# A semaphore wait of GpSimd on VectorE's last SBUF operation, in an attention and MoE kernel

## The chip, the cores and the metric

The kernel runs on one core of a Trainium2 chip. The metric is the device time of one execution in microseconds (us). Five engines take part: TensorE (PE, its weight loads PEld), VectorE (DVE), ScalarE (ACT), GpSimd (POOL), and SyncE (SP), which issues all DMAs. Each engine works through its own queue in order and meets the others only through semaphores. Half a per cent of the time is 3.7 us.

## What is computed

Attention over 4 batches of 8 heads, 576 positions, head size 64, with rotated queries and keys; its output is the input of a two-layer block on 2304 tokens, all in float32.

```python
scores = scale * np.matmul(rotate(q), rotate(k).transpose(0, 1, 3, 2))
attn = np.exp(scores - np.max(scores, axis=-1, keepdims=True))
attn = attn / (np.sum(attn, axis=-1, keepdims=True) + 1e-09)
x = np.matmul(attn, v).transpose(0, 2, 1, 3).reshape(2304, 512)
h = x @ w_in                                  # 512 -> 2048
out = (h * (1.0 / (1.0 + np.exp(-1.702 * h)))) @ w_out   # 2048 -> 512
```

## The kernel before

Heads go in 16 pairs. For each pair, `prep` loads q and k (RAW tiles), turns them by three `combine` operations with the tables `cos_sin_sb` (a product into BT, a product in RAW, a sum into RAW; all L354), and transposes them on TensorE (L475). The transposed tiles become KP for the first four pairs, and for the others KA, KB, QT and QZ, split into a high and a low part (L349 or L351, and L519). `scores` multiplies them into PSUM (SPS; L607, L627). `softened` copies a row negated with its least value on VectorE (L646), and ScalarE takes the exponential (L649, into PP or PJ). The weights are transposed (PT; L709, L804, L837, L882), copied to PW or PH and multiplied with v (AV). The sums of the rows are inverted (ST; L680 adds, L681 inverts, L684 transposes), and the output tile XS is scaled and split into two parts and written to `x_dram`.

The second block goes in 9 chunks of 256 tokens and 16 slices of the inner size. TensorE computes h from XC and win (L1038), ScalarE the tanh (L1044), VectorE the product T (L1046); T is copied (G, high part, L341 to L345) and subtracted (G, low part, L354), and TensorE multiplies by wout (L1055). The weights win and wout arrive as 64-bit words and are converted by integer steps on tiles CW or CV: L992 and L994 on ScalarE, L996, L998 and L1001 on VectorE, an integer add on GpSimd (L1004), a cast (L341 or L343) and a subtraction (L354).

No operation is issued in the order of the source. Every one is given to a `Plan` with its engines, durations, buffers and a priority, and `Plan.order` works out a timetable at build time; the operations are then issued in the order of their planned starts. `vec` marks each with a `port`: `(POOL, DVE)` for an operation on SBUF alone, `(POOL,)` for one that reads PSUM. In the timetable two operations that carry a port with their own engine in it do not overlap:

```python
if e in o.port and port_at > t + 1e-9:
    at(port_at, e, o)
    continue
```

On the chip this is not enforced: before the change the only waits are those that data and buffers need. `copy` (L339) and `combine` (L353) are the helpers that most operations on GpSimd go through, so the profile shows lines L345 and L354 for many different tiles. The last loop of the kernel (L1098) issues the operations.

Of the kernel before, what the change touches and what calls it, by code (L numbers as in the profile page):

```python
# [15 lines left out]
ALU = mybir.AluOpType  # L16
# [30 lines left out]
PE, ACT, DVE, POOL, SP = "PE", "ACT", "DVE", "POOL", "SP"  # L47
# [234 lines left out]
def attention_moe(ctx: ExitStack, tc: tile.TileContext, q, k, v, w_in, w_out, cos_sin, out):  # L282
    nc = tc.nc
# [53 lines left out]
    engine = {ACT: nc.scalar, DVE: nc.vector, POOL: nc.gpsimd}  # L337

    def copy(e, to, src):  # L339
        if e == ACT:  # L340
            nc.scalar.copy(to, src)  # L341
        elif e == DVE:
            nc.vector.tensor_copy(to, src)  # L343
        else:
            nc.gpsimd.tensor_scalar(to, src, 1.0, 1.0, op0=ALU.mult, op1=ALU.mult)  # L345

    def scaled(e, to, src, by):
        if e == ACT:
# [2 lines left out]
            nc.vector.tensor_scalar(to, src, by, None, op0=ALU.mult)  # L351

    def combine(e, to, a, b, how):  # L353
        engine[e].tensor_tensor(to, a, b, op=how)  # L354

    def dma(fn, nbytes, *deps, full=0, part=0, row=2048, land=900.0, **kw):

# [18 lines left out]
    def make_tiles(pool, counts):  # L376
        for p, n in counts.items():
            at = base.get(p, 0)
            for i in range(at, at + n):
                plan.tiles[p][i] = pool.tile(shape[p][0], shape[p][1], name=f"{p}{i}")  # L380

    def open_pool(name, side, counts=None):
        pool = tc.tile_pool(name=name, bufs=1, side=side, reuse_waits="tile")
        tiles = pool.__enter__()
        make_tiles(tiles, counts or {})
        return pool, tiles
# [40 lines left out]
    def prep_qk(n, s, prio):  # L427
# [18 lines left out]
        if n in plain_qk:  # L446
            def f():
                for h in range(2):
# [3 lines left out]
                    else:  # L452
                        for i, src in enumerate((q, k)):
# [7 lines left out]
        rope = "POOL DVE" if n or s == 1 else "DVE POOL"  # L461
        heads = lambda t: t.rearrange("p t c (a d) -> p t (c a) d", a=2)
        o = vec(rope, "two", w, lambda e: combine(e, halves(bt.t[:, 0:n_t]), halves(raw.t)[:, :, :, ::-1, :], sn,
                                                  ALU.mult), ld, tables, bufs=[raw, bt], prio=prio + at["rope"])
        o = vec(rope, "two", w, lambda e: combine(e, heads(raw.t), heads(raw.t), cs, ALU.mult), o, bufs=[raw],
                prio=prio + at["rope"])
        added = n < at["n_added"]
        if not added:
            o = vec(rope, "two", w, lambda e: combine(e, raw.t, raw.t, bt.t[:, 0:n_t], ALU.add), o, bufs=[raw, bt],
                    prio=prio + at["rope"])  # L470
# [61 lines left out]
    def prep(n):  # L532
# [40 lines left out]
        for h in range(2):  # L573
            vs = plan.buf("VS")
            pr = p0 + at["v_split"] + (0 if h == 0 else PAIR_LEN[n] / 3)
            hi = vec("ACT POOL", "sbuf", 5 * D, lambda e, h=h, vs=vs: copy(e, vs.t[:, :, 0, :], raw.t[:, h]), ld,
                     bufs=[raw, vs], prio=pr)
            lo = vec("POOL DVE", "two", 5 * D, lambda e, h=h, vs=vs: combine(
                e, vs.t[:, :, 1, :], raw.t[:, h], vs.t[:, :, 0, :], ALU.subtract), hi, bufs=[raw, vs], prio=pr)
            vs_of[n].append(vs)  # L580
            vs_ready[n].append(lo)
# [91 lines left out]
    def inverse_sums(n, tiles, exps, xs, prio):  # L673

        st, pt, rt = st_of[n], pt_buf(n), buf("RT")
        c0, k = column_of[n].index(tiles[0]), len(tiles)

        def f():
            a = st.t[:, 1, c0:c0 + k]
            nc.vector.tensor_scalar(a, a, 1e-9, None, op0=ALU.add)  # L680
            nc.vector.reciprocal(a, a)  # L681

        o = op(DVE, 330.0, f, exps, bufs=[st], prio=prio)
        o = pe(lambda: nc.tensor.transpose(pt.t[0:k, 0:128], st.t[:, 1, c0:c0 + k], ident), o, tr=[128],  # L684
               bufs=[st, pt, rt], prio=prio)
        o = vec("ACT DVE", "psum", 128, lambda e: copy(e, rt.t[0:k], pt.t[0:k, 0:128]), o, bufs=[pt, rt], prio=prio)
        o = dma(lambda: nc.sync.dma_start(r_dram[n, c0:c0 + k], rt.t[0:k]), 4600, o, full=1, bufs=[rt], prio=prio)

        heads = [[t for t in tiles if t < 4], [t for t in tiles if t > 4]]
        row = lambda t: column_of[n].index(t) * 128  # L690
        pieces = [(0, 128 * heads[0][0], row(heads[0][0]), 128 * len(heads[0]) + 64 * (4 in tiles)),
                  (64, 128 * heads[0][0], row(heads[1][0]), 128 * len(heads[1]))]
        if 4 in tiles:
            pieces.append((64, 512, row(4) + 64, 64))

        def f():
            rows = r_dram[n].rearrange("(a t) p -> a (t p)", a=1)
            for r0, to, at, w in pieces:
                nc.sync.dma_start(xs.t[r0:r0 + 64, 0, to:to + w], rows[:, at:at + w].to_broadcast([64, w]))

        return dma(f, 34000.0 * k, o, part=len(pieces), land=1350.0, bufs=[xs], prio=prio)
# [14 lines left out]
    def split(pt, ph, ready, parts, prio):  # L716

        done = []
        for r0, r1, c0, c1, to in parts:
            w = c1 - c0  # L720
            src = lambda r0=r0, r1=r1, c0=c0, c1=c1: pt.t[r0:r1, c0:c1]
            part = lambda l, to=to, w=w, tall=r1 - r0 == 128: (
                ph.t[:, 512 * l + to:512 * l + to + w] if tall else ph.t[64 * l:64 * l + 64, to:to + w])
            hi = vec("ACT DVE", "psum", w, lambda e, src=src, part=part: copy(e, part(0), src()), ready, bufs=[pt, ph],
                     prio=prio + at["copy_p"], chain="turned")
            done.append(vec("DVE", "psum", w, lambda e, src=src, part=part: nc.vector.tensor_tensor(  # L726
                part(1), src(), part(0), op=ALU.subtract), hi, bufs=[pt, ph], prio=prio + at["copy_p"]))
        return done
# [366 lines left out]
    with tc.manual_schedule():  # L1095
        mid, _ = open_pool("mid", "right", MID)
        left, _ = open_pool("early", "left", early)
        for o in plan.order():  # L1098
            if mid and any(b.pool in LATER for b in o.bufs):
                mid.__exit__(None, None, None)  # L1100
                mid = None
                later = ctx.enter_context(tc.tile_pool(name="later", bufs=1, side="right", reuse_waits="tile"))
                make_tiles(later, LATER)
            if left and first_late <= o.idx < last_late:
                left.__exit__(None, None, None)
                left = None
                late = ctx.enter_context(tc.tile_pool(name="late", bufs=1, side="left", reuse_waits="tile"))
                win[1] = late.tile([128, 2, KD, DFF // 2], F32R, name="win1")
                wout[1] = late.tile([128, 2, KH, DM], F32R, name="wout1")
            o.fn(o.eng)  # L1110


# [38 lines left out]
```

## Time and profile before

| | |
|---|---|
| time, median of 3 runs | 740.62 us (739.92 to 742.65) |
| the profiled execution | 742.06 us |
| its span in the trace | 740.3 us |
| busy, TensorE / VectorE / ScalarE / GpSimd | 707.0 / 501.4 / 421.1 / 254.1 us |
| operations, VectorE / GpSimd | 1168 / 297 |

The span is the time from the first to the last instruction in the trace; the rest of the execution's time lies around it. An engine's busy time is the sum of its instructions' durations, overlaps counted once. An instruction that stands still inside its execution counts as busy, so a long duration of a form that is short elsewhere is a sign of such a stand. Idle time in square brackets at a row is that of the engine just before it, with what ended it. Later sections name the stretches by the trace's time in us.

### The profile page before, as it was taken

What the parts mean: (1) busy time and instruction counts of PE and PEld (TensorE: products, weight loads), DVE (VectorE), ACT (ScalarE), POOL (GpSimd) and SP (SyncE); (2) the same over time, 40 slices, a digit from 0 to 9 for tenths busy, and PEclk for the clock granted to TensorE, in tenths of its full rate; (3) what the DMA queues carried; (4) which work ended last, traced back from release to release, by engine and by line L of the source; (5) the groups of instructions that cost most, each with busy time, mean ns of one, the idle gap of its engine ahead of it and who ended that gap; (6) DMA issues with size and microseconds to landing.
All of it is one profiled execution on the core that took longest, in us unless ns stands there. A gap on an engine that the chain in (4) does not pass through costs nothing.

```text
span 740.3 us, 14104 instructions
## 1 busy us (share of the span) xinstructions
PE 707.0 (95%) x4921; PEld 618.0 (83%) x4921; DVE 501.4 (68%) x1168; ACT 421.1 (57%) x1038; POOL 254.1 (34%) x297
## 2 busy tenths in 40 slices
PE   6899797999999999999999999999999999999997
PEld 4566475878887898999999999899999998999996
DVE  5999999888889886477788788788752222222322
ACT  3677896666867764466666666766653232322322
POOL 4687765455456434144143433432110000000000
PEclk7999998999999999999999999999999999999999
DMA  7545647555455544222232343521103020100000
GB/s 174 143 104 163 187 141 207 176 161 148 134 169 155 165 137 116 93 73 70 63 99 67 93 120 97 126 66 44 38 17 118 1 86 0 60 28 1 29 1 29
DMA packets 103335, 72.16 MB, mean 97 GB/s; under 512 B 67536, under 2 KB 88032, under 8 KB 103264
## 3 DMA queue, kind: packets, MB, share of 16 engines
q1 hardware_dynamic: 103264, 71.26, 34.0%
q8 instruction: 39, 0.64, 0.4%
q14 instruction: 32, 0.26, 0.1%
HBM read 48.87 MB, written 15.28 MB: 87 GB/s over the span
## 4 chain that ended last, share of the span: by engine, by line
PE 80%; DVE 9%; ACT 4%; DMA 3%; issue 2%; POOL 1%; SPq 1%; ACTq 0%; DVEq 0%; POOLq 0%
PE PT L1038 26%; PE SPS L1055 25%; PE SPS L607 8%; PE AV L737 5%; PE PT L709 5%; PE SPS L627 2%; PE PT L882 2%; PE PT L804 1%; PE AV L895 1%; PE PT L475 1%; DVE PP L646 1%; PE AV L819 1%; DMA RAW<-in_k_dram 1%; ACT PP L649 1%; DVE RAW L354 1%
## 5 line engine op out<-in xcount | busy, mean ns | idle before, releaser
L1038 PE MATMUL PT<-XC,win 128*128 128x256 f32 x1728 | 242.3, 286 | 0.2
L1038 PEld LDWEIGHTS PT<-XC,win 128*128 128x128 f32 x1728 | 227.2, 191 | 9.3 <-DVE T L1046 1.3
L1055 PE MATMUL SPS<-wout,G 128*128 128x512 f32 x864 | 234.4, 400 | 0.3 <-ACT G L341 0.3
L1055 PEld LDWEIGHTS SPS<-wout,G 128*128 128x128 f32 x864 | 150.5, 189 | 23.3 <-ACT G L341 0.7
L1046 DVE SCALAR_TENSOR_TENSOR T<-T,PT 128x256 f32<-128x256 f32 x144 | 60.4, 419 | 90.9 <-ACT T L1044 89.6
L1044 ACT ACTIVATE T<-PT 128x256 f32<-128x256 f32 x144 | 55.1, 383 | 113.7 <-PE PT L1038 105.7
L649 ACT ACTIVATE PP<-PP,ST 128x576 f32<-128x576 f32 x128 | 99.3, 777 | 24.2 <-DVE PP L646 23.2
L646 DVE TENSOR_SCALAR_CACHE_REDUCE PP<-SPS 128x576 f32<-128x576 f32 x128 | 94.9, 750 | 21.1 <-PE SPS L607 16.5
L354 DVE TENSOR_TENSOR G<-T,G 128x256 fp32r<-128x256 f32 x117 | 54.8, 468 | 61.4 <-ACT G L341 55.0
L341 ACT CAST G<-T 128x256 fp32r<-128x256 f32 x115 | 46.6, 405 | 64.4 <-PE SPS L1055 61.2
L345 POOL TENSOR_SCALAR G<-T 128x256 fp32r<-128x256 f32 x29 | 11.9, 412 | 203.7 <-PE SPS L1055 154.9
L726 DVE TENSOR_TENSOR PH<-PT,PH 128x512 fp32r<-128x512 f32 (+4 forms) x128 | 65.7, 528 | 19.3 <-ACT PH L341 17.4
L341 ACT CAST PH<-PT 128x512 fp32r<-128x512 f32 (+4 forms) x115 | 50.9, 457 | 33.8 <-PE PT L709 29.3
L737 PE MATMUL AV<-PH,VS 128*128 128x256 f32 (+2 forms) x368 | 62.4, 289 | 0.0
L737 PEld LDWEIGHTS AV<-PH,VS 128*128 128x128 f32 x368 | 53.2, 189 | 1.5
L354 POOL TENSOR_TENSOR BT<-RAW,cos_sin_sb 128x512 f32<-128x512 f32 (+1 forms) x33 | 32.8, 994 | 46.2 <-DMA RAW<-in_k_dram 42.4
L709 PE MATMUL PT<-ident,PP 128*128 128x128 f32 x288 | 48.2, 277 | 0.1
L354 POOL TENSOR_TENSOR RAW<-RAW,BT 128x512 f32<-128x512 f32 (+1 forms) x36 | 36.2, 1006 | 12.5 <-DVE RAW L354 8.3
L1004 POOL TENSOR_TENSOR CV<-CV 128x256 int32<-128x256 int32 x32 | 25.2, 789 | 38.7 <-DVE CV L1001 33.5
L709 PEld LDWEIGHTS PT<-ident,PP 128*128 128x128 f32 x288 | 33.9, 140 | 4.4 <-DVE QZ L519 1.2
L607 PE MATMUL SPS<-KB,QT 128*128 128x288 f32 x192 | 35.9, 308 | 0.9 <-DVE PJ L646 0.8
L341 ACT COPY PW<-PT 128x512 f32<-128x512 f32 (+2 forms) x59 | 29.4, 516 | 11.7 <-PE PT L882 9.0
(123 smaller groups left out, 1023.0 us busy)
## 6 DMA issues: line engine op xcount, KB each, us to landing
XC<-x_dram SPq DMA_DIRECT2D x22, 512.0 KB
x_dram<-XS SPq DMA_DIRECT2D x15, 576.0 KB
out_dram<-O SPq DMA_DIRECT2D x18, 256.0 KB
RAW<-in_q_dram SPq DMA_DIRECT2D x32, 128.0 KB
RAW<-in_k_dram SPq DMA_DIRECT2D x32, 128.0 KB
OW<-in_moe_w_in_dram SPq DMA_DIRECT2D x8, 512.0 KB
OW<-in_moe_w_out_dram SPq DMA_DIRECT2D x8, 512.0 KB
O<-in_moe_w_in_dram SPq DMA_DIRECT2D x16, 256.0 KB
```

The source lines that it names most:

```text
L341: nc.scalar.copy(to, src)
L354: engine[e].tensor_tensor(to, a, b, op=how)
L607: nc.tensor.matmul(s.t[:, c, to:to + wid], w, kt.t[:, l, at:at + wid], start=(i == l == 0), stop=(i == len(kts) - 1 and l == 1 and to + wi ...
L646: o = vec("DVE", "psum", S, lambda e: nc.vector.tensor_scalar(to().rearrange("p (c s) -> p c s", c=2), s.t[:, :, 0:HALF], -1.0, LARGEST, o ...
L649: return vec("ACT", "sbuf", S, lambda e: nc.scalar.activation(to(), to(), AF.Exp, bias=st.t[:, 0, col:col + 1], scale=-1.0, accum_out=st.t ...
L709: nc.tensor.transpose(pt.t[0:w, to:to + r], p.t[r0:r0 + r, c0:c0 + w], ident[r0:r0 + r, r0:r0 + r])
L726: done.append(vec("DVE", "psum", w, lambda e, src=src, part=part: nc.vector.tensor_tensor(part(1), src(), part(0), op=ALU.subtract), hi, b ...
L737: nc.tensor.matmul(av.t[:, to:to + w], vs[h].t[:, kt].rearrange("p a d -> p (a d)"), ph.t[:, 512 * l + at:512 * l + at + w], start=(first ...
L1038: nc.tensor.matmul(h.t[:, 0:CT], win[f_i // KH][:, wl, kk, f_i % KH * 128:(f_i % KH + 1) * 128], xc[xl].t[:, kk, :], start=(i == m == 0), ...
L1044: o = vec("ACT", "psum", CT, lambda e, h=h, t=t: nc.scalar.activation(t.t, h.t[:, 0:CT], AF.Tanh, scale=gate), o, bufs=[h, t], prio=pr + a ...
L1046: o = vec("DVE", "psum", CT, lambda e, h=h, t=t: nc.vector.scalar_tensor_tensor(t.t, t.t, 1.0, h.t[:, 0:CT], op0=ALU.add, op1=ALU.mult), o ...
L1055: nc.tensor.matmul(acc.t[:, m, :], g.t[:, a, m * 128:(m + 1) * 128], wout[f_i // KH][:, b, f_i % KH, :], start=(f_i == fs[0] and i == 0), ...
```

## The change

Two helpers hand back the instruction that they issue. The issuing loop remembers the last VectorE instruction that was issued with DVE in its port (`holder`), and gives each later GpSimd instruction with POOL in its port a semaphore dependency on it. The operations, their engines and their order stay as they are. VectorE is given no wait on GpSimd. Lines after the first edit are one less in the changed file (L353 is L354 of before).

```diff
@@ -338,11 +338,10 @@
 
     def copy(e, to, src):
         if e == ACT:
-            nc.scalar.copy(to, src)
-        elif e == DVE:
-            nc.vector.tensor_copy(to, src)
-        else:
-            nc.gpsimd.tensor_scalar(to, src, 1.0, 1.0, op0=ALU.mult, op1=ALU.mult)
+            return nc.scalar.copy(to, src)
+        if e == DVE:
+            return nc.vector.tensor_copy(to, src)
+        return nc.gpsimd.tensor_scalar(to, src, 1.0, 1.0, op0=ALU.mult, op1=ALU.mult)
 
     def scaled(e, to, src, by):
         if e == ACT:
@@ -351,7 +350,7 @@
             nc.vector.tensor_scalar(to, src, by, None, op0=ALU.mult)
 
     def combine(e, to, a, b, how):
-        engine[e].tensor_tensor(to, a, b, op=how)
+        return engine[e].tensor_tensor(to, a, b, op=how)
 
     def dma(fn, nbytes, *deps, full=0, part=0, row=2048, land=900.0, **kw):
 
@@ -1095,6 +1094,7 @@
     with tc.manual_schedule():
         mid, _ = open_pool("mid", "right", MID)
         left, _ = open_pool("early", "left", early)
+        holder = None
         for o in plan.order():
             if mid and any(b.pool in LATER for b in o.bufs):
                 mid.__exit__(None, None, None)
@@ -1107,7 +1107,12 @@
                 late = ctx.enter_context(tc.tile_pool(name="late", bufs=1, side="left", reuse_waits="tile"))
                 win[1] = late.tile([128, 2, KD, DFF // 2], F32R, name="win1")
                 wout[1] = late.tile([128, 2, KH, DM], F32R, name="wout1")
-            o.fn(o.eng)
+            done = o.fn(o.eng)
+            if o.eng == POOL and POOL in o.port and holder is not None:
+                tc.add_manual_dep(done.ins, holder.ins.name, mybir.DependencyInfo(
+                    mybir.DependencyClass.Sync, mybir.DependencyReason.DATA), reason="the port that DVE and POOL share")
+            elif o.eng == DVE and DVE in o.port:
+                holder = done
 
 
 # ---- launch: one core; inputs and outputs as the reference has them ----
```

What the semaphores of GpSimd's queue are in the two programs is shown at two places. The names behind "waits" are the semaphores: DMAHW0 to DMAHW7 of DMAs, and those of the engines (Activation is ScalarE). The first place is GpSimd's queue at 22 to 28 us, where RAW and BT belong to the turning of q and k. Before:

```order
L354 TENSOR_TENSOR RAW_125<-RAW_125,BT_75 128x128 [waits Pool_49]
L354 TENSOR_TENSOR BT_126<-RAW_73,cos_sin_sb 128x512 [waits DMAHW5_49,DMAHW4_49]
L354 TENSOR_TENSOR RAW_72<-RAW_72,BT_75 128x512 [waits DMAHW6_49,DVE_49,PE_49]
L354 TENSOR_TENSOR BT_75<-RAW_74,cos_sin_sb 128x128 [waits DMAHW6_49,DMAHW1_49,DMAHW7_49,DMAHW0_49,Pool_49]
L354 TENSOR_TENSOR RAW_73<-RAW_73,BT_126 128x512 [waits DVE_49,PE_49]
```

The same five after the change:

```order
L353 TENSOR_TENSOR RAW_125<-RAW_125,BT_75 128x128 [waits Pool_49]
L353 TENSOR_TENSOR BT_126<-RAW_73,cos_sin_sb 128x512 [waits DMAHW5_49,DMAHW4_49,DVE_49]
L353 TENSOR_TENSOR RAW_72<-RAW_72,BT_75 128x512 [waits DMAHW6_49,PE_49]
L353 TENSOR_TENSOR BT_75<-RAW_74,cos_sin_sb 128x128 [waits DMAHW1_49,DMAHW6_49,DMAHW0_49,DMAHW7_49,DVE_49,Pool_49]
L353 TENSOR_TENSOR RAW_73<-RAW_73,BT_126 128x512 [waits PE_49]
```

Nothing moved in the queue. Both products into BT wait for VectorE (DVE) now and did not before; the sums behind them lose the wait, since the queue is already past it.

The second place is GpSimd's queue at 83 to 92 us, from an integer add of the weights over a subtraction into wout to the turning of a pair and its XS. Before:

```order
L1004 TENSOR_TENSOR CW_135<-CW_135 128x512 [waits DVE_49,Activation_49]
L354 TENSOR_TENSOR wout_62<-CW_134,wout_62 128x512 [waits Activation_49]
L354 TENSOR_TENSOR BT_75<-RAW_73,cos_sin_sb 128x512 [waits DMAHW6_49,DMAHW5_49]
L354 TENSOR_TENSOR RAW_73<-RAW_73,cos_sin_sb 128x512 [waits PE_49,Pool_49]
L354 TENSOR_TENSOR XS_87<-XS_87 128x576 [waits DMAHW2_49,DMAHW3_49,DMAHW1_49,Activation_49]
L354 TENSOR_TENSOR RAW_73<-RAW_73,BT_75 128x512 [waits Pool_49]
```

After:

```order
L1003 TENSOR_TENSOR CW_135<-CW_135 128x512 [waits Activation_49]
L353 TENSOR_TENSOR wout_62<-CW_134,wout_62 128x512 [waits Activation_49]
L353 TENSOR_TENSOR BT_75<-RAW_73,cos_sin_sb 128x512 [waits DMAHW6_49,DMAHW5_49,DVE_49]
L353 TENSOR_TENSOR RAW_73<-RAW_73,cos_sin_sb 128x512 [waits PE_49,Pool_49]
L353 TENSOR_TENSOR XS_87<-XS_87 128x576 [waits DMAHW2_49,DMAHW3_49,DMAHW1_49,Activation_49]
L353 TENSOR_TENSOR RAW_73<-RAW_73,BT_75 128x512 [waits Pool_49]
```

The product into BT has a wait on VectorE that it did not have, and the first add here has lost its own, because the add in front of it waits further now.

## Rows read from the trace of the kernel before

**Rows 1.** The page: busy us (share of the span) xinstructions, by engine.

```profile
PE 707.0 (95%) x4921; PEld 618.0 (83%) x4921; DVE 501.4 (68%) x1168; ACT 421.1 (57%) x1038; POOL 254.1 (34%) x297
```

**Rows 2.** Stretches: us, busy (xcount) of PE, PEld, DVE, ACT, POOL, PEclk, DMA share, GB/s.

```profile
22.00:120.00 98.00, 87.60 (x670) 58.77 (x670) 93.04 (x204) 78.19 (x187) 70.24 (x59) 1.00 0.55 152
120.00:240.00 120.00, 111.03 (x797) 95.00 (x796) 103.63 (x246) 84.03 (x217) 64.13 (x79) 0.96 0.55 160
240.00:600.00 360.00, 358.44 (x2550) 331.66 (x2549) 251.28 (x596) 210.91 (x522) 108.15 (x133) 1.00 0.31 85
...
123.20:130.00 6.80, 6.08 (x28) 5.75 (x29) 5.95 (x12) 2.74 (x8) 2.54 (x2) 0.50 0.59 157
```

**Rows 3.** TensorE's waits, 22 to 240 us: us in total, times, longest us.

```profile
PE PT L882 <- DVE QZ L519: 3.4, 3, 1.9
```

**Rows 4.** Timeline, VectorE, 95 us: start, duration (us), line, operation, tiles, form, count.

```profile
95.35 0.76 DVE L996 TENSOR_SCALAR CW<-CW 128x512 f32<-128x512 f32 x2
```

**Rows 5.** Timeline, VectorE, then GpSimd, then TensorE, 22 to 28 us.

```profile
22.81 1.76 DVE L354 TENSOR_TENSOR BT<-RAW,cos_sin_sb 128x512 f32<-128x512 f32 x1
25.10 0.68 DVE L354 TENSOR_TENSOR RAW<-RAW,cos_sin_sb 128x512 f32<-128x512 f32 x1
...
27.05 0.68 DVE L343 COPY PW<-PT 128x512 f32<-128x512 f32 x1
27.66 0.41 DVE L996 TENSOR_SCALAR CW<-CW 128x512 f32<-128x512 f32 x1
...
22.52 1.50 POOL L354 TENSOR_TENSOR BT<-RAW,cos_sin_sb 128x512 f32<-128x512 f32 x1
25.91 1.27 POOL L354 TENSOR_TENSOR RAW<-RAW,BT 128x512 f32<-128x512 f32 x1 [1.89 <-PE PT L804]
...
27.84 0.63 PE L475 MATMUL PT<-ident,RAW 128*128 128x128 f32 x4 [1.96 <-POOL BT L354]
```

**Rows 6.** Timeline, VectorE, then GpSimd, then TensorE, 86 to 91 us.

```profile
86.97 1.24 DVE L354 TENSOR_TENSOR win<-CW,win 128x512 fp32r<-128x512 f32 x1
88.13 1.82 DVE L354 TENSOR_TENSOR XS<-XS 128x576 f32<-128x576 f32 x1
...
86.39 1.26 POOL L354 TENSOR_TENSOR BT<-RAW,cos_sin_sb 128x512 f32<-128x512 f32 x1
87.73 1.61 POOL L354 TENSOR_TENSOR RAW<-RAW,cos_sin_sb 128x512 f32<-128x512 f32 x1
...
90.31 0.27 PE L684 MATMUL PT<-ident,ST 128*4 128x128 f32 x1 [1.38 <-DVE ST L681]
```

**Rows 7.** Timeline, VectorE, then GpSimd, 55 to 59 us.

```profile
55.66 1.28 DVE L1001 SCALAR_TENSOR_TENSOR CW<-OW,CW 128x512 int32<-128x512 int32 x2
...
56.42 2.88 POOL L1004 TENSOR_TENSOR CW<-CW 128x512 int32<-128x512 int32 x2 [1.64 <-DVE CW L1001]
```

**Rows 8.** Timeline, VectorE, then GpSimd, then TensorE, 119 to 124 us.

```profile
119.64 1.55 DVE L354 TENSOR_TENSOR XS<-XS 128x320 fp32r<-128x320 f32 x1
121.12 1.75 DVE L354 TENSOR_TENSOR BT<-RAW,cos_sin_sb 128x512 f32<-128x512 f32 x1
...
119.20 3.12 POOL L1004 TENSOR_TENSOR CW<-CW 128x512 int32<-128x512 int32 x2 [2.71 <-DVE CW L1001]
...
123.92 1.11 PE L882 MATMUL PT<-ident,PP 128*128 128x128 f32 x4 [1.85 <-DVE QZ L519]
```

**Rows 9.** Timeline, VectorE, then TensorE, 200 to 207 us.

```profile
200.78 0.29 DVE L998 TENSOR_SCALAR CV<-CV 128x256 int32<-128x256 int32 x1
...
201.90 0.97 DVE L354 TENSOR_TENSOR G<-T,G 128x256 fp32r<-128x256 f32 x1
202.79 1.37 DVE L998 TENSOR_SCALAR CV<-CV 128x256 int32<-128x256 int32 x1
...
206.12 0.66 PE L882 MATMUL PT<-ident,PP 128*128 128x128 f32 x4 [1.27 <-DVE QT L519]
```

**Rows 10.** ScalarE's waits, whole span: us in total, times, longest us.

```profile
ACT win L341 <- POOL CW L1004: 1.9, 2, 1.6
```

## The prediction

> **What bounds the kernel now.** I read the page's busy line first: TensorE is busy for 707.0 of 740.3 us [rows 1]. At best some 33 us can be had, and they have to be looked for where TensorE is idle. The windows come next [rows 2]: from 240 to 600 us it is busy for 358.44 of 360 us, so nothing that VectorE or GpSimd do there is worth anything. From 22 to 120 us it is busy for 87.60 of 98, and from 120 to 240 for 111.03 of 120: 19.4 us of idle time, in the stretch where VectorE works 93.04 of 98 and 103.63 of 120 us. The view of TensorE's waits for 22 to 240 us says whom it waits for: its first row names VectorE [rows 3], and six of its eight largest rows do. So between 22 and 240 us the chain goes through VectorE's queue, and TensorE follows.
>
> Then I went through VectorE's queue beside GpSimd's. An operation that reads and writes SBUF alone has two durations. Two L996 of 128x512 back to back take 0.76 us [rows 4]; the L354 of 128x512 at 25.10 takes 0.68 us, the same form at 22.81 takes 1.76 [rows 5]. The long one began while a GpSimd operation ran and ended about 0.6 us after it: 22.52 + 1.50 = 24.02, and 24.57. At 88.13 it is 1.82 us for 128x576, beside GpSimd's 87.73 + 1.61 = 89.34 [rows 6]. VectorE stands still until GpSimd is through, then does its work. Operations that read PSUM do not show this: L646 and L1046 take the same time beside GpSimd or alone. Summed over all SBUF operations, form by form against the undisturbed ones, VectorE stands still for about 31 us.
>
> **What the change does to each side.** Of 278 planned GpSimd operations, 76 get a wait for a VectorE instruction later than any they waited for. I laid each beside the trace: in 19 that instruction was long done (the wait is free); in 31 it was running; in 26 it had not begun. Nothing else moves on any engine.
>
> *The 31 in flight.* GpSimd starts, finds the port taken, and goes on when VectorE ends. With the wait it starts after the semaphore instead. At 55.66 two L1001 end at 56.94; GpSimd's two adds run from 56.42 for 2.88 us, to 59.30 [rows 7]. Begun at about 57.02 (0.08 for the semaphore, the least distance seen from VectorE's end to GpSimd's start), with two undisturbed adds of 1.27 (the duration of the RAW add at 25.91, the same size [rows 5]), they would end at 59.56: 0.26 us later. That is 0.2 to 0.3 us each, 31 times, on an engine that is busy 70.24 of 98 and 64.13 of 120 us [rows 2]; GpSimd's next idle time hides it. Without that cover its consumers pay, see the second rival. At this very place VectorE gains, too: L680 behind the pair no longer meets a running add.
>
> *The 26 not begun.* Here GpSimd now lets VectorE go first. By my sum over these places 18.7 of the 31 us of standing still go away on VectorE. What it is worth is read from the TensorE gap that follows, and no place can give more than its gap:
> - **22 to 28 us.** GpSimd's BT at 22.52 waits for the L354 of 25.10 [rows 5]. VectorE's 22.81 loses 1.08 us of waiting, all behind it comes 1.08 earlier, and BT starts at 24.71 + 0.08. It ends at 26.06, and the RAW add behind it at 27.33 instead of 27.18. The wait before 27.84 is put down to GpSimd's BT of 27.25, which is no input of that operation; by its semaphores it needs the RAW add and the PW copy that ends at 27.73. The copy is then done at 26.66, so the add decides: 0.4 us. The L996 of 27.66, undisturbed before, now begins at 26.58 inside the add and waits to 27.33: 0.75 of the 1.08 is given back to the rest of the queue.
> - **86 to 90 us.** BT at 86.39 waits for the XS of 88.13; win loses 1.24 - 0.68 = 0.56, XS 1.82 - 0.76 = 1.06 (0.76 from 0.68 by size). TensorE's gap before 90.31 is 1.38 and ends on this chain: all 1.38 go [rows 6].
> - **119 to 124 us.** The two adds of 119.20 wait for the BT of 121.12 and for a later one. The BT loses 1.75 - 0.68 = 1.07 and the XS as much; the four small operations behind them (the last one releases TensorE) come 2.1 earlier, and the gap before 123.92 is 1.85: 1.85 [rows 8].
> - **201 to 206 us.** The G of 201.90 loses 0.97 - 0.42 = 0.55, the L998 of 202.79 loses 1.37 - 0.29 = 1.08 (0.29 is the L998 at 200.78, 0.42 the undisturbed mean of this G form); the gap before 206.12 is 1.27: 1.27 [rows 9].
> - **The same pattern** at six more gaps, before 44.80, 58.41, 145.11, 168.22 (with 165.95), 233.99 and 238.19: 0.70, 0.36, 0.25, 1.11, 0.54 and 0.34, by the smaller of gap and lost wait: 3.3.
>
> Sum: 0.4 + 1.38 + 1.85 + 1.27 + 3.3 = 8.2 us. Against it stands what comes back. A GpSimd operation that starts later can meet a VectorE operation that it did not meet before, since VectorE waits for nothing new. Of the places walked above, one in four shows it clearly, for 0.75. With 26 delayed operations, and on the average half of that on the chain for one in four, I take 2.2 us. Bounds: nothing comes back (0), all comes back (8.2). The value is nearer the low end because the operation next in VectorE's queue issues before the semaphore reaches GpSimd, so only the second one behind is in danger.
>
> **GpSimd's results** come later by up to 2.8 us at the 26 places. Measured from each of its instructions along all that wait for it to the next TensorE start, the distance is larger nearly everywhere (at 22.52 it is 1.9 against a delay of 2.0, at 119 it is 4.4 against 1.2). I cost this at nothing; the cover is that GpSimd works half to two thirds of the time there.
>
> **The clock** is granted at 0.50 (1.2 of 2.4 GHz) from 123.2 to 130.0, right behind the gap of 1.85 us, with 6.08 us of TensorE work in it [rows 2]. At the upper level that work would take 3.0 us less. I count none of it in the value and all of it in the low end.
>
> **Rivals.**
> *The port only changes hands.* What VectorE gains, GpSimd loses, and its later operations stop VectorE elsewhere, as the L996 at 26.58 will. For it: 12.3 of the 31 us stand behind operations that get no useful wait, so such meetings are common. Against: GpSimd has idle time at every one of the four places, and VectorE has none. The price is the whole 8.2: 740.6, or 738 to 742 with a part of it. The Trainium skill, "SBUF — State Buffer", § Who interferes with whom, states this as a rule: the pair is an exclusive lock for the whole instruction, and issue order decides who blocks. The rows at 22.81 and 88.13 agree, and by that rule alone the port's total work stays, which speaks for this rival.
>
> *The integer adds hold ScalarE's queue* (slower). 48 adds of the weights (L1004) run on GpSimd, most get a wait. ScalarE's cast behind each waits at the head of its queue with the exponentials of the softmax behind it, and TensorE needs those. It waits so now, 1.9 us in two waits for one of the tiles [rows 10]. With 0.26 us for each of 48, 12.5 us, and half of it reaching TensorE, that is +6.2: 746.8. It decides where the time between add and cast is under 0.2 us and ScalarE has no idle time; it has, 78.19 of 98 and 84.03 of 120 us are busy [rows 2].
>
> *The change does nothing* would need all waits to be met already; 26 are not, so this has no chance of its own.
>
> **How the numbers follow.** The profiled execution took 742.06 us, its span being 740.3; the median of the three runs is 740.62, 1.4 below it. 742.06 - 8.2 + 2.2 = 736.1 for that execution, and with the same 6.0 us off the median 734.6. Forecast (a gain of 3.7 us or more, since 0.5%, or 3.7 us, is about the least that a measurement of this kernel tells from no change): 0.62, from 729.5 (all 8.2 and the clock's 3.0) to 736.9. The port only changes hands, or much of it: 0.28, 737 to 742. The adds hold ScalarE: 0.10, 744 to 748. Range for 8 in 10: 729.5 to 741.0, leaving out the slower case and the last part of the second. Chances: faster 0.62, same 0.28, slower 0.10.
>
> **What would show it.** In the changed profile VectorE's busy time in 22 to 240 us should fall by 10 to 18 us while its count stays; the XS at 88 and the BT at 121 should read 0.7 to 0.8; the gaps before the operations now at 90.31, 123.92 and 206.12 should be gone; GpSimd's adds should read 1.27 where they read 1.6, with more idle time before them named after VectorE. If VectorE's busy time falls and the span does not, new waits on GpSimd's results stand in TensorE's or ScalarE's view. If it does not fall, the first rival is right. I am wrong altogether if TensorE waits on win, wout or G.

## The result

The change takes 732.7 us (median of 6 runs, 730.45 to 736.52); before takes 742.01 us beside it (6 runs, 739.92 to 743.0). The ratio is 0.9883, 95% interval 0.9852 to 0.9913: faster by some 8.7 us, 6.5 to 11.0 (the ratio goes by all runs, not by the two medians, which lie 9.3 apart). The forecast was 6.0 us. The profiled execution took 731.63 us with a span of 729.9, 10.4 less than the span of before. Lines of after are one less than those of before: L353 is L354 there.

The page of after, busy us by engine, answers [rows 1]:

```profile
PE 704.7 (97%) x4921; PEld 617.4 (85%) x4921; DVE 491.7 (67%) x1168; ACT 421.6 (58%) x1038; POOL 246.1 (34%) x297
```

VectorE does the same 1168 operations in 9.7 us less, GpSimd its 297 in 8.0 us less, and TensorE's share rises. The stretches answer [rows 2]; columns as there:

```profile
22.00:120.00 98.00, 91.41 (x687) 62.79 (x686) 91.06 (x213) 80.62 (x192) 66.48 (x60) 0.96 0.57 160
120.00:240.00 120.00, 115.09 (x869) 98.61 (x868) 104.76 (x257) 88.79 (x232) 66.77 (x83) 1.00 0.58 167
240.00:600.00 360.00, 358.63 (x2530) 332.71 (x2529) 246.24 (x584) 207.65 (x512) 102.05 (x128) 1.00 0.29 83
9.70:26.80 17.10, 13.01 (x45) 8.87 (x46) 12.36 (x29) 9.46 (x22) 9.38 (x9) 0.50 0.86 208
84.80:88.20 3.40, 3.40 (x14) 2.29 (x13) 3.09 (x9) 3.40 (x7) 2.23 (x2) 0.50 0.96 218
118.80:125.60 6.80, 5.66 (x43) 4.82 (x42) 6.36 (x12) 3.79 (x9) 4.43 (x5) 1.00 0.85 214
```

A stretch of before that [rows 2] leaves out and that after does not have at the lower level either:

```profile
167.50:171.00 3.50, 2.78 (x11) 2.41 (x12) 2.85 (x6) 1.63 (x5) 1.99 (x4) 0.51 0.63 145
```

Between 22 and 240 us TensorE is idle for 11.5 us (98 - 91.41 + 120 - 115.09) where it was 19.4: 7.9 us of the 10.4. From 240 to 600 TensorE's busy time did not change, as [rows 2] said. The stretch that answers 123.2 to 130.0 of before is 118.8 to 125.6; its granted clock is 1.00 instead of 0.50. But after has a stretch at 0.50 of its own at 84.8, and the one near the start lasts to 26.8 (in before to 20.8).

Below is the timeline of after at the four places: VectorE, GpSimd and TensorE (start, duration, line, operation, idle before), place by place, answering [rows 5], [rows 6], [rows 8] and [rows 9].

```profile
24.12 0.68 DVE L353 TENSOR_TENSOR RAW<-RAW,cos_sin_sb 128x512 f32<-128x512 f32 x1
...
27.05 0.63 DVE L995 TENSOR_SCALAR CW<-CW 128x512 f32<-128x512 f32 x1
...
24.88 1.27 POOL L353 TENSOR_TENSOR BT<-RAW,cos_sin_sb 128x512 f32<-128x512 f32 x1 [2.17 <-DVE RAW L353]
26.11 1.28 POOL L353 TENSOR_TENSOR RAW<-RAW,BT 128x512 f32<-128x512 f32 x1
...
27.45 0.66 PE L474 MATMUL PT<-ident,RAW 128*128 128x128 f32 x4
...
84.45 0.69 DVE L353 TENSOR_TENSOR win<-CW,win 128x512 fp32r<-128x512 f32 x1
85.06 0.75 DVE L353 TENSOR_TENSOR XS<-XS 128x576 f32<-128x576 f32 x1
...
85.89 1.27 POOL L353 TENSOR_TENSOR BT<-RAW,cos_sin_sb 128x512 f32<-128x512 f32 x1 [1.70 <-DVE ST L679]
...
87.52 0.42 PE L683 MATMUL PT<-ident,ST 128*4 128x128 f32 x1
...
116.54 0.49 DVE L353 TENSOR_TENSOR XS<-XS 128x320 fp32r<-128x320 f32 x1
116.94 0.69 DVE L353 TENSOR_TENSOR BT<-RAW,cos_sin_sb 128x512 f32<-128x512 f32 x1
...
117.70 1.27 POOL L1003 TENSOR_TENSOR CW<-CW 128x512 int32<-128x512 int32 x1 [4.10 <-DVE BT L353]
...
118.80 0.60 PE L881 MATMUL PT<-ident,PP 128*128 128x128 f32 x4
...
193.74 0.41 DVE L353 TENSOR_TENSOR G<-T,G 128x256 fp32r<-128x256 f32 x1
194.08 0.28 DVE L997 TENSOR_SCALAR CV<-CV 128x256 int32<-128x256 int32 x1
...
195.94 1.04 PE L881 MATMUL PT<-ident,PP 128*128 128x128 f32 x8
```

XS takes 0.75 us (1.82 before), BT 0.69 (1.75), G 0.41 (0.97), L997 0.28 (1.37). GpSimd's idle time before its BT and its add is now named after VectorE, and the TensorE operations that stood behind gaps of 1.38 and 1.85 us have none in front of them; the one that stood behind 1.27 us is the fifth of the eight at 195.94, which follow one another without a gap. The L995 at 27.05 still stands 0.22 us, behind the add that ends at 27.39.

### The profile page after: what moved, and what is told of

Its sections match the earlier page's. It is cut to its first block, busy times and chain, and to the rows that moved or that the text cites. A ratio compares the mean times of both kernels' runs of the same rounds, so it can differ in the third digit from the quotient of the medians.

```text
span 729.9 us, 14109 instructions
## 1 busy us (share of the span) xinstructions
PE 704.7 (97%) x4921; PEld 617.4 (85%) x4921; DVE 491.7 (67%) x1168; ACT 421.6 (58%) x1038; POOL 246.1 (34%) x297
## 3 DMA queue, kind: packets, MB, share of 16 engines
q1 hardware_dynamic: 103264, 71.26, 34.6%
## 4 chain that ended last, share of the span: by engine, by line
PE 83%; DVE 8%; ACT 4%; issue 2%; DMA 1%; POOL 1%; SPq 1%; ACTq 0%; DVEq 0%; POOLq 0%
PE PT L1037 26%; PE SPS L1054 25%; PE SPS L606 8%; PE AV L736 6%; PE PT L708 5%; PE SPS L626 3%; PE PT L803 2%; PE PT L881 2%; PE AV L818 2%; PE AV L894 1%; PE PT L474 1%; DVE PP L645 1%; ACT PP L648 1%; ACT PW L341 1%; DVE QT L518 1%
## 5 line engine op out<-in xcount | busy, mean ns | idle before, releaser
L353 DVE TENSOR_TENSOR G<-T,G 128x256 fp32r<-128x256 f32 x117 | 54.4, 465 | 61.3 <-ACT G L341 55.0
L353 POOL TENSOR_TENSOR BT<-RAW,cos_sin_sb 128x512 f32<-128x512 f32 (+1 forms) x33 | 32.5, 986 | 52.1 <-DMA RAW<-in_k_dram 23.8
L353 POOL TENSOR_TENSOR RAW<-RAW,BT 128x512 f32<-128x512 f32 (+1 forms) x36 | 36.4, 1010 | 7.7 <-DVE RAW L353 5.0
L626 PE MATMUL SPS<-KP 64*128 64x288 f32 (+3 forms) x168 | 30.8, 465 | 4.5 <-DVE PP L645 3.8
```

Source lines behind the costliest of these rows:

```text
L353: return engine[e].tensor_tensor(to, a, b, op=how)
```

## Experiments

All kernels do the same operations in the same order as the change; only the waits differ. A GpSimd operation's turn is its number, from 0, among the 278 that the plan issues. "Standing still" is, as in the prediction, the sum over VectorE's SBUF operations of duration less the undisturbed one of the form: 31.1 us before, 20.0 after. What is taken as undisturbed moves these sums by up to 1.7 us.

**The 26 waits alone, and all others.** The turns in the set are the 26 GpSimd operations whose VectorE instruction had not begun in the trace of before. In the second kernel those turns take no wait of their own, nor one by which the next turn would make up for it.

```diff
-            if o.eng == POOL and POOL in o.port and holder is not None:
+            if o.eng == POOL and POOL in o.port:
+                turn += 1
+                if holder is not None and turn in BEGUN_LATE:   # 26 turns
```

> Only the 26 waits whose VectorE instruction had not begun in the trace of before are kept. Theory (VectorE no longer stands still behind those GpSimd operations): nearly the whole gain, 8 us of the 8.7 measured, so a ratio of 0.988 to 0.990 against the kernel before, the gaps of TensorE before 90.3, 123.9 and 206.1 gone. Rival (the semaphore step lets VectorE's next operation go first everywhere, the running ones count as much): about half, 4 us, a ratio near 0.995.

> All waits but those 26. Theory: 0 to 1 us (at 58 us the small L680 behind a pair of L1001 gets ahead of the add, worth the 0.36 us gap), a ratio of 0.998 to 1.000, VectorE's busy time down by 1 to 2 us. Rival (semaphore step): 4 us or more, near 0.994. If it is slower than 1.002 the running waits cost, and the 26 alone are the better kernel.

The 26 take 734.1 us, ratio 0.9908 (0.9879 to 0.9938); the others 741.46, 1.0003 (0.9987 to 1.0019). So the gain comes from the waits on operations not begun; the free and the in-flight ones together give or cost less than these runs resolve, about 1.4 us. The page of the 26, busy us by engine:

```profile
PE 704.2 (96%) x4921; PEld 616.9 (84%) x4921; DVE 489.9 (67%) x1168; ACT 420.9 (58%) x1038; POOL 250.7 (34%) x297
```

And that of the others:

```profile
PE 708.8 (96%) x4921; PEld 618.9 (84%) x4921; DVE 500.8 (68%) x1168; ACT 421.8 (57%) x1038; POOL 251.2 (34%) x297
```

VectorE's busy time falls by 11.5 us with the 26 and by 0.6 with the others; standing still is 18.2 and 30.3 us. With the others alone the stands of [rows 6] and [rows 9] are back, and TensorE's gap behind the second:

```profile
89.08 1.82 DVE L353 TENSOR_TENSOR XS<-XS 128x576 f32<-128x576 f32 x1
...
202.45 1.38 DVE L997 TENSOR_SCALAR CV<-CV 128x256 int32<-128x256 int32 x1
...
205.77 0.66 PE L881 MATMUL PT<-ident,PP 128*128 128x128 f32 x4 [1.28 <-DVE QT L518]
```

The gap before the operation that was at 44.80 is there, too, with the others (0.97 us) and gone with the 26. Two places are less clear. Before the operation of 123.92 the gap is gone in both profiles: with the others VectorE got in first there without a wait (see the last section), and a stretch at 0.50 from 118.9 to 122.3 took up part of it. Before that of 58.41 it is 0.18 with the 26 and gone with the others, so that term belongs at least in part to the waits in flight.

**Five waits at the four places** of the prediction: turns 8 (BT at 22.52), 47 (BT at 86.39), 64 and 65 (the adds of 119.20), 113 (at 201).

```diff
+        PLACES = {8, 47, 64, 65, 113}
+                if holder is not None and turn in PLACES:
```

> Five waits only: the product BT at 22.52, the product BT at 86.39, the two adds at 119.20 and 120.81, the add at 201.86. Theory: the sum of the terms of those four places, 0.4 + 1.38 + 1.85 + 1.27 = 4.9 us, with up to 1 us more for a stretch at the upper clock level behind 124 us: 736.1 to 737.1 beside 742.0, a ratio of 0.992 to 0.994. Rival (the gain is in where the low clock falls): the gain follows the mean granted clock, not the places, and can be anything from 0 to 5 us.

737.62 us, 0.9956 (0.993 to 0.9981): 3.3 us (1.4 to 5.2), less than expected. The terms of the prediction stand in its trace where they were put: TensorE gains 1.44 us at the operation that was at 90.31 (forecast 1.38), 2.01 at that of 123.92 (1.85), 1.44 at that of 206.12 (1.27). Five waits of 278 carry about two fifths of the gain. But its runs scatter over 6.7 us, and they go by the mean granted clock: the five at 0.985 and 0.986 take 735.04 to 737.22 us (the profiled one is the shortest), the four at 0.974 and 0.975 take 740.86 to 741.76, where before, at 0.973 and 0.974, takes 741.22 to 742.33 beside it. At the low clock the five waits gain next to nothing, so the rival that the gain follows the clock is not excluded for this kernel. For the 26 it is: 736.21 us in the run at 0.977, where before takes 742.43 to 743.70 at 0.977 and 0.978.

**ScalarE as a stand-in.** GpSimd's operations wait for the last planned ScalarE operation on SBUF or PSUM: a delay that has nothing to do with VectorE.

```diff
-            elif o.eng == DVE and DVE in o.port:
+            elif o.eng == ACT and o.port:
                 holder = done
```

> The control: each GpSimd operation waits for the last ScalarE operation that the plan has in front, not for VectorE. GpSimd is held back in much the same way, the port goes to whoever comes. Theory: no gain, VectorE still stands still for some 31 us, 741 to 745 us, a ratio of 1.000 to 1.005. Rival (a later GpSimd helps whatever it waits for): faster by 3 us or more, below 0.996.

749.62 us, 1.0121 (1.0087 to 1.0155). A later GpSimd as such does not help; it costs more than I expected. Standing still rises to 39.1 us. At the places of the prediction, though, this delay does what the change does: the XS of 88.13 takes 0.75 us in its profile, the BT of 121.12 0.68 and the L998 of 202.79 0.29, and TensorE has no gap before the operation of 206.12. The loss is made elsewhere, most of it behind 240 us: by the starts of the same TensorE operations the kernel is 2.2 us behind before at 260 us and 7.5 at 600.

**The other side waits.** VectorE's SBUF operations wait for the last GpSimd operation that the plan has in front, and GpSimd waits for nothing new; then both.

```diff
-            if o.eng == POOL and POOL in o.port and holder is not None:
+            if o.eng == DVE and DVE in o.port and holder is not None:
                 ...
-            elif o.eng == DVE and DVE in o.port:
+            elif o.eng == POOL and POOL in o.port:
                 holder = done
```

> The wait the other way round: each VectorE operation on SBUF waits for the last GpSimd operation that the plan has in front, GpSimd waits for nothing new. Theory (VectorE's queue is the chain, so it matters who is let through): slower, since VectorE waits for GpSimd operations that have not even begun as well; 745 to 755 us beside 741.6, a ratio of 1.005 to 1.02. Rival (two operations are kept apart, in whichever order): faster like the change, below 0.995.

> Both waits, so that the plan's order of the port is kept exactly. Theory: VectorE never stands still behind a running GpSimd operation, but waits for it by semaphore, and for those not begun too; the change's gain of 7 to 9 us less the loss of the reversed wait, 735 to 750 us, slower than the change alone by at least 4. Rival (keeping the plan is what gains): at or below the change, 0.988 or less.

VectorE waiting takes 742.92 us, 1.0036 (1.0016 to 1.0056), slower as expected, though by less (1.005 to 1.02); both 739.18, 0.9975 (0.9955 to 0.9994). The timeline of the first shows why, VectorE and then TensorE at the place of 88.13:

```profile
90.24 1.82 DVE L353 TENSOR_TENSOR XS<-XS 128x576 f32<-128x576 f32 x1
...
92.42 0.27 PE L683 MATMUL PT<-ident,ST 128*4 128x128 f32 x1 [1.55 <-DVE ST L680]
```

The XS still stands for a microsecond and TensorE's gap is still there: in the plan GpSimd's BT comes behind this XS, so VectorE has no reason to wait for it, and on the chip BT is early. With both sides waiting, standing still is down to 1.7 us and VectorE's busy time to 474.2, the lowest of all, and yet it is slower than the change. What it stood before it waits now. VectorE's waits there (us in total, times, longest):

```profile
DVE CW L995 <- POOL RAW L353: 5.0, 6, 1.5
DVE G L353 <- POOL RAW L353: 4.3, 5, 1.8
...
DVE G L353 <- POOL win L353: 2.8, 4, 0.9
```

So VectorE's busy time alone is no measure of the gain: a stand that becomes a semaphore wait leaves the busy time and stays in the queue. The kernel in which VectorE alone waits says the same: its VectorE is busy for 492.6 us, hardly more than in the change (491.7), and it gains nothing.

**Waiting for any VectorE operation.** The holder is VectorE's last operation with any port, so those that read PSUM count too. At 242 of the 278 turns that is a later instruction than in the change.

```diff
-            elif o.eng == DVE and DVE in o.port:
+            elif o.eng == DVE and o.port:
                 holder = done
```

> GpSimd waits for the last planned VectorE operation of any kind, those that read PSUM too, which do not meet GpSimd. Theory: no more to gain (TensorE's gaps that are left at 84, 112 to 118 and 160 do not end on a VectorE operation that stands still), and GpSimd's results come later still: 0 to 6 us slower than the change, a ratio of 0.988 to 0.997. Rival (the more GpSimd yields the better): faster than the change, 0.985 or less.

754.22 us, 1.0182 (1.016 to 1.0203): far off what I expected, 21.5 us over the change, the slowest of all. Standing still is 37.9 us. Two causes offered themselves. GpSimd is released where VectorE's next SBUF operation begins and meets it (standing still), or its results come late for those who need them. The next two kernels split the 242 turns by what VectorE does next.

```diff
+                before = last if DVE in follows[n] else holder   # 56 turns; the second kernel: "not in", 186 turns
...
+            elif o.eng == DVE and o.port:
+                last = done
+                holder = done if DVE in o.port else holder
```

> As the change, but where VectorE's last operation in the plan reads PSUM and its next one is on SBUF alone (56 of the 278 GpSimd operations), GpSimd waits for that PSUM operation. Waiting for any VectorE operation at all 242 places where that is a later one took 1.0182 of before, 21.5 us over the change, with 37.9 us of standing still on VectorE instead of 20.0. Theory (the loss is standing still: GpSimd is released just as VectorE's next SBUF operation begins, and loses the time beside the PSUM operation in which the port was free): these 56 carry most of it, 12 us or more over the change: 744 to 752, 1.003 to 1.014, with 30 us or more of standing still. Rival (the loss is that GpSimd's results come late, whatever VectorE does next): 56 of 242 places, 23% of 21.5 us, 5 us over the change: 736 to 740, 0.992 to 0.998.

> The complement: GpSimd waits for VectorE's last PSUM operation only where the next one reads PSUM as well (186 of the 278 operations), and elsewhere as in the change. Theory (the loss is standing still): most of these are released beside another PSUM operation, standing still stays within 20 to 25 us, and at most 8 us are lost to the change: 733 to 741, 0.988 to 0.999. Rival (late results of GpSimd): 186 of 242 places, 77% of 21.5 us, 16 us over the change: 746 to 752, 1.005 to 1.014.

The 56 turns take 738.22 us, 0.9963 (0.9947 to 0.9978), 5.5 over the change's median; the 186 take 748.82, 1.0116 (1.0097 to 1.0135), 16.1 over it. These are the rival's numbers (5 and 16): in these two kernels the loss goes by the number of delayed operations, and my theory of the next operation fell. Standing still is 22.3 and 35.8 us. In the first it is only 2.3 over the change, which does not account for its 5.5 us; there lateness must have a part. In the second, 15.8 over, the two are not told apart. Where the lateness lands shows in ScalarE's waits on GpSimd (us in total, times, longest). Before, beside [rows 10]:

```profile
ACT T L1044 <- POOL G L354: 2.6, 4, 1.1
...
ACT wout L341 <- POOL CV L1004: 0.9, 2, 0.7
ACT win L341 <- POOL CV L1004: 0.8, 3, 0.3
```

After:

```profile
ACT win L341 <- POOL CV L1003: 4.9, 9, 1.6
ACT win L341 <- POOL CW L1003: 3.7, 3, 2.7
ACT T L1043 <- POOL G L353: 2.4, 4, 1.1
```

The 186 turns:

```profile
ACT T L1042 <- POOL G L352: 9.5, 8, 2.7
ACT win L341 <- POOL CV L1002: 8.6, 12, 1.8
ACT wout L341 <- POOL CV L1002: 5.5, 7, 1.5
```

Summed over all tiles ScalarE waits for GpSimd 7.0 us before, 14.6 with the change, 21.9 and 34.6 in these two, 40.9 with all 242. And much of the loss is made where before has no idle time of TensorE: from 260 to 600 us, by the starts of the same TensorE operations, the 56 turns lose 1.3 us against before, the 186 lose 6.4 and the 242 lose 6.9, while the change gains 0.5. TensorE's gaps there are 1.7, 3.4 and 3.2 us, 1.6 in before, so most of that lies inside what the profile counts as TensorE's busy time.

**The first half of the program.** The change's waits for the first 143 turns, which lie before 240 us; none behind.

```diff
+                if holder is not None and turn < 143:
```

> The change's waits for the first 143 GpSimd operations only, those that ran before 240 us; none later. Theory (TensorE has no idle time from 240 to 600 us, so nothing there counts): the whole gain, a ratio of 0.987 to 0.991, and the same lead of TensorE at 260 us and at the end. Rival (part of the lead of 10 us in the changed profile is made after 240): at least 1 us less, with VectorE's stands at 392 us and behind showing in TensorE's waits.

734.38 us, 0.9915 (0.9889 to 0.9942). The gain is made before 240 us, as [rows 2] said. The interval overlaps that of the change (and so does that of the 26 alone), so the times leave open whether the later waits add the last 1 to 2 us. The profiles do not show that they do: TensorE is ahead of before by 7.7 us at 260 and 9.1 at 600 without them, by 9.9 and 10.4 with them, so the two differ before the later waits come. No kernel beat the change.

## Why the prediction held, and where it was off

**The mechanism and the side were right.** VectorE stood behind GpSimd, the wait on operations not begun lets it go first, and TensorE's gaps behind it close. The split into the 26 and the others puts the gain where the prediction put it. The ScalarE stand-in shows that a delay at every turn does not do it, though at these places it clears the same stands: what counts is to delay there and not elsewhere.

**The terms.** For each place, by how much after gets further ahead there, by the starts of the same TensorE operations in both traces (at 44.80 over the whole group; at 27.84 how far it is ahead, 0.39, less the 0.07 by which VectorE's queue was ahead at 22 us already, since after is at 0.50 for longer and TensorE behind until then, which the wait of 1.96 us of [rows 5] takes up):

| TensorE's operation, at (before) | forecast | measured |
|---|---|---|
| 27.84 | 0.4 | 0.32 |
| 44.80 | 0.70 | 1.4 |
| 58.41 | 0.36 | 0.43 |
| 90.31 | 1.38 | 1.44 |
| 123.92 | 1.85 | 2.02 |
| 145.11 | 0.25 | 0.40 |
| 165.95 and 168.22 | 1.11 | 1.37 |
| 206.12 | 1.27 | 1.44 |
| 233.99 and 238.19 | 0.88 | 0.2 |
| sum | 8.2 | 9.0 |

The largest misses are the last row and the place of 44.80. The row of before is eight matmuls that take 1.91 us behind a gap of 0.70; in after the same eight take 1.24 behind none. TensorE's timeline of before:

```profile
44.80 1.91 PE L627 MATMUL SPS<-KP 64*128 64x288 f32 x8 [0.70 <-DVE PP L646]
```

After:

```profile
43.38 1.24 PE L626 MATMUL SPS<-KP 64*128 64x288 f32 x8
```

Half of that wait lay between the matmuls of one group, where the profile counts it as busy: the third of the eight starts at 45.48, just behind VectorE's second L646 (44.67 + 0.75). "No place can give more than its gap" was too strict: 0.67 us were hidden in the group. At 233.99 nothing came (its gap was 0.51, less than the 0.54 counted, and is 0.50), at 238.19 0.16, and after has a new gap of 0.28 before the operation of 234.40. The change was not tried at these two places alone.

At 22 us even the steps came out: BT forecast at 24.79, measured 24.88; the RAW add's end forecast at 27.33, measured 27.39. The L995 behind it stood 0.22 us, not the forecast 0.75, mainly because VectorE had first to wait 0.29 us for TensorE.

**What comes back** was put at 2.2 us, and here the size is luck. The product behind it, 26 operations, one in four, half of 0.75, is 2.4. New gaps of TensorE in after, or the growth of old ones, before the operations that stood at 76.86, 126.54, 127.72, 129.12, 168.39, 185.28 and 234.40, are 0.27, 0.54, 0.37, 0.20, 0.27, 0.35 and 0.28: 2.3. But the mechanism of the prediction, a later GpSimd that stops VectorE, stands behind the one at 129.12 alone, where a VectorE operation of 0.69 us takes 1.03. At 185.28 a late GpSimd holds ScalarE, whose wait for XS grows from 0.27 to 0.65 us. At the other five TensorE has merely run up to the next ScalarE or VectorE operation, which comes no further behind in its own queue than before. On VectorE itself the mechanism is there: the 26 waits took 12.9 us of standing still away, where the places alone would give 18.7. Little of that reaches TensorE.

**The clock.** The prediction counted none of the 3.0 us of the stretch at 123.2; that stretch begins inside the gap of 1.85 us, not behind it, and the one at 167.5 was not counted. By the starts of the same operations TensorE gets further ahead by 0.9 us from the operation of 123.92 to 130, and by 0.8 from that of 168.22 to 171, where before was at 0.50 and after at 1.00, with four of the new gaps in these stretches. At 84.8, where after is at 0.50, it loses 1.2 us, just before the term of 90.31. The longer stretch at the start costs nothing behind 27.84. So the clock gave some 0.5 us in this pair, though the mean granted clock is 0.986 in both traces: where a stretch falls counts.

Summed up, 9.0 less the 0.9 of the new gaps outside those stretches, with 0.5 from the clock, 0.65 that come after 460 us and the 0.07 at the start, is 9.3 of the 10.4 by which the spans differ. The other 1.1 I can't put down place by place.

The two profiles have an equal mean clock; the runs have not. The six of after show 0.984 on average, the 45 of before that were timed beside the experiments 0.979. At equal clock, 0.979, 0.981, 0.984 and 0.988, the runs of after take 736.52, 733.35, 733.94 and 732.05 us, and those of before 742.1, 740.2, 741.8 and 740.3 (means of 2, 4, 1 and 1): 5.6 to 8.3 less. The gain is there at every level, and the forecast of 6.0 lies in it; up to 3 us of the 8.7 may be the clock's, and these runs do not separate it.

**What the working had wrong beside that.** GpSimd's results were costed at nothing because the distance to the next TensorE start is larger than the delay, but the first example given, 1.9 against 2.0, is smaller. And that nothing between 240 and 600 us is worth anything holds for what can be gained there, not for what can be lost: see the 186 and the 242 turns.

**In-flight waits.** Forecast: 0.26 us later for the pair of adds, hidden. VectorE and then GpSimd in after, answering [rows 7]:

```profile
53.35 1.28 DVE L1000 SCALAR_TENSOR_TENSOR CW<-OW,CW 128x512 int32<-128x512 int32 x2
54.55 0.16 DVE L679 TENSOR_SCALAR ST<-ST 128x9 f32<-128x9 f32 x1
...
54.71 2.51 POOL L1003 TENSOR_TENSOR CW<-CW 128x512 int32<-128x512 int32 x2 [2.24 <-DVE ST L679]
```

The adds end 2.59 us after VectorE's pair (57.22 against 54.63), before 2.36 (59.30 against 56.94): 0.23 later, the adds at 1.26 each. The kernel of the other waits shows that all of them together cost less than can be measured. The idle time before the adds is put down to the L679, which ends at 54.71, as GpSimd starts; 0.08 us after the pair, the distance seen elsewhere, speaks for a wait on the pair.

**The rivals.** *The port only changes hands* did not happen. The rows at 22.81 and 88.13, and now the XS of 1.82 us with VectorE waiting, agree with the rule of the Trainium skill, "SBUF — State Buffer", § Who interferes with whom, that issue order decides who blocks; the place in the last section does not show it so plainly. I had read from it that the total stays. But which of the two blocks is not all the same here: between 22 and 240 us TensorE mostly waits for VectorE, seldom for GpSimd. The three kernels of this pair of engines say so: GpSimd yields 0.9883, VectorE yields 1.0036, both yield 0.9975.

*The adds hold ScalarE's queue* has its mechanism, at a smaller size: ScalarE's waits for GpSimd doubled, 7.0 to 14.6 us, and at 185.28 one of them, on XS and not on an add, reaches TensorE with 0.35 us. The sign for being wrong was a wait of TensorE on win, wout or G. Of its seven largest waits from 22 to 240 us one names G:

```profile
PE PT L683 <- ACT G L341: 1.0, 1, 1.0
```

It is the operation of 168.22, which waited 1.61 us before and waits 1.03 now; ScalarE's cast into G in front of it is not late (166.97 before, 159.99 in after, 6.98 us ahead like the rest of ScalarE's queue there), so this is no late result of GpSimd. With 34.6 and 40.9 us of ScalarE's waits the kernel is slower than before. That cover has an end, and the prediction's 0.10 for this rival rested on ScalarE's idle time alone, which says nothing on how far it reaches.

**Signs that were stated badly.** VectorE's busy time in 22 to 240 us was to fall by 10 to 18 us with the same count. It reads 195.8 against 196.7, but with 470 operations instead of 450, since the program is ahead. By the operation it fell from 0.437 to 0.417 us, 9.6 us for 470. A fixed window is the wrong measure when the program moves through it; the whole span, 501.4 to 491.7, is the better one, and there the fall, 9.7, is just under the low end, since some standing came back.

## What to carry to other kernels

Where VectorE's SBUF operations are long beside GpSimd's, find which of the two the critical engine waits for, and let the other one yield by a semaphore at the operations with which it collides; the plan's order may already say which goes first, while nothing on the chip enforces it. Let it yield to those alone: waiting for VectorE's PSUM operations too cost 21.5 us here, 0.09 for each of the 242 turns on average, and letting both yield gave back most of the gain. A stretch in which the critical engine never idles has nothing to gain from this, but it can lose. Price each place by the gap that closes behind it, and look inside groups of matmuls, too, for waits that count as busy.

## What the runs showed of the hardware

- A GpSimd operation that waited by semaphore started 0.08 us after VectorE's end (24.88 against 24.12 + 0.68). Two undisturbed adds of 128x512 took 2.51 us, and the same pair 2.88 us [rows 7] when it began beside VectorE.
- Which engine gets in first is not settled by which instruction begins first in the trace. With the 26 waits left out, at the place of 119.20, VectorE and then GpSimd:

```profile
121.73 0.49 DVE L353 TENSOR_TENSOR XS<-XS 128x320 fp32r<-128x320 f32 x1
122.13 0.69 DVE L353 TENSOR_TENSOR BT<-RAW,cos_sin_sb 128x512 f32<-128x512 f32 x1
...
121.29 3.88 POOL L1003 TENSOR_TENSOR CW<-CW 128x512 int32<-128x512 int32 x2 [2.71 <-DVE CW L1000]
```

The adds began 0.44 us ahead of XS, exactly as in [rows 8], and while the same pair of VectorE operations in front of XS still ran. In before XS and BT stood (1.55 and 1.75 us) and the adds took 3.12; here XS and BT ran undisturbed and the adds took 3.88, 1.37 more than the pair of 2.51. What decides it stays open, and so does whether one kernel goes the same way in each execution, since there is one trace of each. With the wait of the change GpSimd does not begin before VectorE is through (117.70 against 116.94 + 0.69).
